# Fused chunk attention and wave mixer on one core: scores on eight array tiles in four PSUM banks, and the last chunks of two batch pairs in one group

## The chip, the core and the metric

The kernel runs on one core of a Trainium2 chip. The core has a matmul engine (TensorE, PE in the profile) with its weight loads (PEld), VectorE (DVE), ScalarE (ACT), GpSimd (POOL) and SyncE (SP); each works through its own list of instructions in order and waits on semaphores for the others. Sixteen DMA engines move data between HBM and SBUF; transfers are issued from the queues of SP, ACT and POOL. TensorE writes to PSUM, eight banks of 512 fp32 values on each of 128 partitions. The metric is the device time of one execution in microseconds, the median of the runs shown. The profile is that of one execution more.

## The reference

Attention inside chunks of 64 tokens, and then a mixer on its result. Batch 8, 8 heads, 576 tokens, 64 values per head: nine chunks for each batch and head.

```python
scores = (q_c @ k_c.transpose) / sqrt(64)          # per batch, head and chunk: 64 x 64
attn = softmax(scores); x = attn @ v_c             # x: (8, 576, 512), heads side by side
theta = x @ w_theta                                # 512 x 512
zr, zi = x * cos(theta), x * sin(theta)
y = w_tok_r @ zr + w_tok_i @ zi                    # over the tokens: 576 x 576
u = x + y
out = u + relu(u @ w_ch)                           # 512 x 512
```

Inputs and output are fp32; the kernel computes in fp16 with fp32 sums, and leaves out the subtraction of the row maximum in the softmax, which it doesn't need for these values.

## The kernel before

The batches are taken in four pairs p = 0 to 3. The 2 x 576 tokens of a pair make nine tiles j = 0 to 8 of 128 tokens: 0 to 3 are the first 512 tokens of the first batch, 4 to 7 those of the second, and tile 8 holds the last 64 tokens of both. For the attention a pair is cut into five groups (`GROUPS`): A and B (tiles 0,1 and 2,3), C and D (4,5 and 6,7), and M (tile 8, the last chunks).

A group goes through these steps, each a short name:

- `qk`: q and k are loaded by GpSimd's queue, cast to fp16 on the way, with two tokens and eight heads on a partition (L174; M: L169). For 0A alone q and k come as fp32 by SP's queue (`hq`, `hk`) and are cast on ScalarE and VectorE (`cqa`, `ckv`). `v`: v by GpSimd's queue (L214).
- `T` (or `Tq`, `Tk`): VectorE transposes blocks of 32 x 32 (L321), so that pairs of head values lie on the partitions: two values of one partition are the two terms e = 0, 1 of a sum in PSUM.
- `S`: scores (L339), 64 matmuls of 32 rows by 64 columns in a full group, 32 in an M group. The 128 x 128 array is used in tiles of 32 rows and 64 columns, of which there are eight. A full group uses four of them and two PSUM banks, an M group two. `S0` and `S1` are halves by heads.
- `E`: the exponential (L365, ScalarE). `V0`, `V1`: the products with v and a column of ones, four heads each (L382, four array tiles of 64 x 64). `N0`, `N1`: division by the sum on VectorE (L397, L399), which writes x.
- `X`: x is transposed on TensorE (L419) and copied (`xa` ScalarE, `xv` VectorE), or transposed by DMA (`xd`, SP's queue). `H`: theta (L457). `G`: cos and sin (L476). `Z`: zr and zi (L492 to L499).
- per tile then `Y` (or its parts `Ya`, `Yb`, `Ym`): the mixing over tokens (L522); `A`: + x (L534); `U` with `ua`, `uv`, or `ud`: transposed u, by TensorE or by DMA; `W`: the last matmul (L562); `R`: relu and sum (L574); `st`, `sa`: the store from SP's or ACT's queue.

`TW` transposes the token weights loaded by `lw`; `lt`, `cta` load and cast w_theta; `lc` loads w_ch. ScalarE holds one table of functions at a time; E and G need different ones, and `table` (L144) loads the other when it changes.

Nothing is scheduled at run time: the string `ORDER` lists all steps, and each engine gets its instructions in that order. A step is written `S.1A.6`: step, pair and group (or tile), and a last number, which for TensorE's steps is the first PSUM bank, for loads and other buffers the slot. `dm.21.7` is 21 dummy matmuls of 512 columns into bank 7, which keep TensorE busy where the order expects it to wait (32 in all, 21 of them first). A step that writes a bank waits until the last reader of the bank is done, a load until the last reader of its slot is done. Of the transfers that one queue issues, eight have a semaphore each at a time: the ninth waits in the queue until the first has landed.

## Time and profile before

| | |
|---|---|
| median of 3 runs (lowest, highest) | 194.25 us (193.74, 196.09) |
| the profiled execution, and its span | 192.63 us, 190.9 us |
| granted TensorE clock | 0.999 |
| TensorE, VectorE, ScalarE, GpSimd busy | 94%, 72%, 53%, 44% of the span |
| score matmuls (L339) | 1152, 13.7 us busy |
| dummies (L158) | 32, 10.6 us busy |

"Span" is the time from the first to the last instruction. In a list of groups or a timeline a row names line, engine and operation, output and inputs, partitions x elements, and how many; "[2.50 <-DVE T L321]" is idle time of the engine just before, and what ended it. Matmuls overlap and each has its full length on record (some 0.19 us for a small one), so a run of them is as long as its row less what the last one runs on alone. A row of windows gives a stretch and its length, then for each engine its busy time and the instructions at work in it, then the granted clock, the share of the DMA engines and GB/s.

### The profile page before, as it was taken

What the parts mean: (1) busy time and instruction counts of PE and PEld (TensorE: products, weight loads), DVE (VectorE), ACT (ScalarE), POOL (GpSimd) and SP (SyncE); (2) the same over time, 40 slices, a digit from 0 to 9 for tenths busy, and PEclk for the clock granted to TensorE, in tenths of its full rate; (3) what the DMA queues carried; (4) which work ended last, traced back from release to release, by engine and by line L of the source; (5) the groups of instructions that cost most, each with busy time, mean ns of one, the idle gap of its engine ahead of it and who ended that gap; (6) DMA issues with size and microseconds to landing.
All of it is one profiled execution on the core that took longest, in us unless ns stands there. A gap on an engine that the chain in (4) does not pass through costs nothing.

```text
span 190.9 us, 6053 instructions
## 1 busy us (share of the span) xinstructions
PE 179.3 (94%) x2626; PEld 93.0 (49%) x2626; DVE 136.8 (72%) x254; ACT 100.7 (53%) x129; POOL 84.9 (44%) x119
## 2 busy tenths in 40 slices
PE   7769899999999999998999999999989999999980
PEld 2245555655556555655456555454544444444430
DVE  0167889789958989959788798967771963672761
ACT  3238979399579780499062774996344650000000
POOL 7786988559856997789578400000000000000000
PEclk9999999999999999999999999999999999999999
DMA  5999999999999999999999998632498315256596
GB/s 156 252 225 187 176 172 174 193 132 159 259 199 162 120 162 198 183 173 194 201 228 200 176 163 180 85 86 82 84 87 177 99 55 137 59 192 165 133 319 213
DMA packets 99867, 31.48 MB, mean 165 GB/s; under 512 B 90880, under 2 KB 94848, under 8 KB 99840
## 3 DMA queue, kind: packets, MB, share of 16 engines
q0 software_dynamic: 75152, 15.49, 93.9%
q1 hardware_dynamic: 21936, 10.75, 24.8%
q10 hardware_dynamic: 2752, 4.85, 7.4%
q8 instruction: 20, 0.33, 0.7%
q14 instruction: 7, 0.06, 0.1%
HBM read 33.06 MB, written 9.44 MB: 223 GB/s over the span
## 4 chain that ended last, share of the span: by engine, by line
PE 64%; DMA 17%; POOL 6%; ACT 5%; DVE 3%; issue 3%; DVEq 0%; POOLq 0%
PE psum L522 29%; DMA land<-in_k_dram 15%; PE psum L562 12%; PE psum L457 11%; PE psum L339 4%; POOL v L214 3%; PE psum L382 2%; POOL land L174 2%; DMA uT<-x 2%; PE psum L419 2%; PE psum L539 2%; ACT L144 1%; PE psum L288 1%; DVE T L321 1%; ACT sin L476 1%
## 5 line engine op out<-in xcount | busy, mean ns | idle before, releaser
L522 PEld LDWEIGHTS <-wT 128*128 128x128 f16 (+1 forms) x360 | 31.0, 100 | 34.5 <-issue 1.2
L214 POOL DMA_DIRECT2D v<-in_v_dram x56 | 42.0, 772 | 7.1 <-DMA land<-in_k_dram 4.0
L522 PE MATMUL psum<-zr,wT 128*128 128x512 f16 (+1 forms) x180 | 44.7, 380 | 0.0
L522 PE MATMUL psum<-zi,wT 128*128 128x512 f16 (+1 forms) x180 | 42.9, 379 | 0.0
L534 DVE TENSOR_TENSOR x<-psum,x 128x512 f16<-128x512 f32 x36 | 24.3, 684 | 20.2 <-PE psum L522 20.0
L562 PE MATMUL psum<-wch,uT 128*128 128x512 f16 (+1 forms) x148 | 35.2, 374 | 1.2 <-DMA uT<-x 0.7
L457 PE MATMUL psum<-wtheta,xT 128*128 128x512 f16 x144 | 34.1, 379 | 0.2 <-DVE xT L442 0.2
L321 DVE STREAM_TRANSPOSE T<-land 128x1024 f32<-128x1024 f32 (+4 forms) x27 | 25.4, 953 | 10.0 <-DMA land<-in_q_dram 5.9
L574 DVE SCALAR_TENSOR_TENSOR o<-psum,x 128x512 f32<-128x512 f32 (+1 forms) x37 | 24.1, 670 | 9.3 <-PE psum L562 9.2
L365 ACT ACTIVATE eT<-psum 128x1024 f16<-128x1024 f32 (+1 forms) x22 | 18.2, 860 | 22.7 <-PE psum L339 20.3
L476 ACT ACTIVATE cos<-psum,pihalf 128x1024 f16<-128x1024 f32 (+1 forms) x22 | 21.1, 958 | 12.5 <-PE psum L457 11.4
L399 DVE TENSOR_TENSOR x<-psum,recip 128x512 f16<-128x512 f32 (+1 forms) x40 | 25.5, 638 | 1.4
L144 ACT ACT_TABLE_LOAD x20 | 25.7, 1283 | 1.1 <-PEq L643 0.7
L562 PEld LDWEIGHTS <-uT 128*128 128x128 f16 x148 | 13.6, 98 | 15.8 <-DMA uT<-x 1.5
L457 PEld LDWEIGHTS <-xT 128*128 128x128 f16 x144 | 13.5, 98 | 16.0 <-DVE xT L442 0.6
L476 ACT ACTIVATE sin<-psum 128x1024 f16<-128x1024 f32 (+1 forms) x22 | 19.0, 865 | 0.0
L174 POOL DMA_DIRECT2D land<-in_q_dram x15 | 14.3, 950 | 5.8 <-DMA land<-in_k_dram 2.1
L339 PE MATMUL psum<-T 32*64 32x64 f16 x1152 | 13.7, 193 | 3.3 <-DVE T L321 3.3
L339 PEld LDWEIGHTS <-T 32*64 32x64 f16 x1152 | 11.8, 106 | 7.6 <-DVE T L321 4.3
L174 POOL DMA_DIRECT2D land<-in_k_dram x15 | 13.6, 907 | 1.7 <-DMA land<-in_k_dram 1.5
L492 DVE TENSOR_TENSOR zr<-x,cos 128x1024 f16<-128x1024 f16 (+1 forms) x18 | 11.2, 623 | 1.3 <-ACT cos L476 1.0
L493 DVE TENSOR_TENSOR zi<-x,sin 128x1024 f16<-128x1024 f16 (+1 forms) x18 | 11.3, 627 | 0.8 <-ACT sin L476 0.7
(39 smaller groups left out, 124.9 us busy)
## 6 DMA issues: line engine op xcount, KB each, us to landing
out_dram<-o ACTq DMA_DIRECT2D x17, 256.0 KB, 3.4
land<-in_q_dram POOLq DMA_DIRECT2D x15, 256.0 KB, 6.6
land<-in_k_dram POOLq DMA_DIRECT2D x15, 256.0 KB, 7.9
out_dram<-o SPq DMA_DIRECT2D x14, 256.0 KB, 4.6
v<-in_v_dram POOLq DMA_DIRECT2D x40, 64.0 KB, 6.4
v<-in_v_dram POOLq DMA_DIRECT2D x16, 128.0 KB, 7.2
land<-in_moe_w_theta_dram SPq DMA_DIRECT2D x2, 512.0 KB, 7.1
out_dram<-o SPq DMA_DIRECT2D x7, 128.0 KB, 3.2
```

Of the source, the lines that this page charges most:

```text
L144: nc.scalar.activation(out=first, in_=pihalf, func=func)
L174: nc.gpsimd.dma_start(t[:, w].rearrange("p h s d -> p h (s d)"), ap[2 * p + bb, :, s0 : s0 + GT, :].rearrange("h (p s) d -> p h (s d)", s=2),)
L214: nc.gpsimd.dma_start(v16[rows, slot + t, :, 0:D], v[b, :, t0 : t0 + m, :].rearrange("h s d -> s h d"),)
L321: nc.vector.transpose(to.bitcast(FP32).rearrange("p (x l s) -> p x s l", l=32, s=2), src.bitcast(FP32).rearrange("p (x s d) -> p x s d", s ...
L339: nc.tensor.matmul(ps[half[r ^ cc], r, h - hs[0]], t[quarter[c], 1, h, :, e], t[quarter[c], 0, h, :, e], start=(e == 0), stop=(e == 1), ti ...
L399: nc.vector.tensor_tensor(out=x.rearrange("p r (h d) -> p r h d", h=H // 2), in0=ps[:, :, :, 0:D], in1=recip[:, 0:n].broadcast_to((P, n, H ...
L457: nc.tensor.matmul(ps[:, (j - js[0]) * DM : (j - js[0] + 1) * DM], xT[:, j, a, :], wtheta16[:, a, :], start=(a == 0), stop=(a == NDB - 1),)
L476: nc.scalar.activation(out=t[:, js[0] : js[-1] + 1].rearrange("p j e -> p (j e)"), in_=ps, func=AF.Sin, bias=bias, scale=1.0,)
L522: nc.tensor.matmul(ps[half[c]] if j == MID else ps, wT[:, kt, t0 : min(t0 + P, S)], z, start=(b is not None and i == 0), stop=(i == len(kt ...
L534: nc.vector.tensor_tensor(out=x, in0=st.pop(("ps_y", p, j)), in1=x, op=ALU.add)
L562: nc.tensor.matmul(ps, uT[:, a, :], wch16[:, a, cols[f]], start=(a == 0), stop=(a == NDB - 1),)
L574: nc.vector.scalar_tensor_tensor(out=o, in0=ps, scalar=0.0, in1=st["x", p][:, j, cols[f]], op0=ALU.max, op1=ALU.add,)
```

## The change

- **Loads of q and k.** A full group now has four tokens and four heads on a partition: heads 0 to 3 on partitions 0 to 63, heads 4 to 7 on 64 to 127. So each load is two, one for each half of the partitions, and their runs in HBM are twice as long. An M group keeps two tokens.
- **Transpositions** write with a step of four; q and k of 0A, 0B, 0C and 0D are transposed in one instruction each.
- **Scores.** The 64 matmuls of a full group go to all eight tiles of 32 x 64, in turn, and into four banks (heads half f and tile r choose the bank), half a bank each. `S0`, `S1` are gone; `E0`, `E1` now take the halves of what `S` wrote.
- **Last chunks.** M of pair 2 takes M of pair 3 along (`WITH_NEXT`): one group of four chunks, 64 score matmuls on four tiles, and one step each where there were two. For that, x, zr, zi and v16 are one array each with one tile more (`OWN`), and `place` says where tile j of pair p lies.
- **Dummies** read one zero repeated 512 times. Helpers that no step used are gone.
- **Order.** A new `ORDER`, with 51 dummies: it begins with 0A, then 0M, then 0B.

```diff
+WITH_NEXT = (2,)
+OWN = 1
...
+    heads = [range(H // 2), range(H // 2, H)]
...
+    def place(p, j):
+        return p % 2 * MID + j if j < MID else 2 * MID + (1, 0, 1, 2 * OWN)[p]
+
+    def pairs(p, g):
+        if g != "M":
+            return [p]
+        ps = [p, p + 1] if p in WITH_NEXT else [p]
+        return sorted(ps, key=lambda x: place(x, MID))
...
-            nc.tensor.matmul(banks(b), zeros[:, 0:P], zeros)
+            nc.tensor.matmul(banks(b), zeros, zeros[:, 0:1].broadcast_to((P, DM)))
...
-                nc.gpsimd.dma_start(
-                    t[:, w].rearrange("p h s d -> p h (s d)"),
-                    ap[2 * p + bb, :, s0 : s0 + GT, :].rearrange(
-                        "h (p s) d -> p h (s d)", s=2
-                    ),
-                )
+                for f in range(2):
+                    nc.gpsimd.dma_start(t[half[f], w].rearrange("p (h x) -> p h x", h=H // 2), four(ap, p, g, f))
+
+    def four(ap, p, g, f):
+
+        j0, bb, s0 = GROUPS[g]
+        rows = ap[2 * p + bb, heads[f][0] : heads[f][-1] + 1, s0 : s0 + GT, :]
+        return rows.rearrange("h (p s) d -> p h (s d)", s=4)
...
+            n, s = (CH * size(p, g), 2) if g == "M" else (P, 4)
...
             nc.vector.transpose(
-                to.bitcast(FP32).rearrange("p (x l s) -> p x s l", l=32, s=2),
-                src.bitcast(FP32).rearrange("p (x s d) -> p x s d", s=2, d=32),
+                to.bitcast(FP32).rearrange("p (x l s) -> p x s l", l=32, s=s),
+                src.bitcast(FP32).rearrange("p (x s d) -> p x s d", s=s, d=32),
             )
...
-            for h in hs:
+    def scores(p, g, b):
+        n = size(p, g)
+        if g == "M":
+            ps = banks(b, n).rearrange("p (r f x) -> p f r x", r=n, f=2)
+            t = st["T", p, g].rearrange("p w (h y e) -> p w h y e", h=H, e=2)
+            work = [
+                (quarter[c], half[c // 2 ^ c % 2], c // 2, f, f * (H // 2), slice(0, CH))
+                for c in range(2 * n) for f in range(2)
+            ]
+            work = [[x for x in work if x[3] == f] for f in range(2)]
+        else:
+
+
+            ps = banks(b, 4).rearrange("p (f r x) -> p f r x", r=n, f=2)[:, :, :, 0 : H // 2 * CH]
+            t = st["T", p, g].rearrange("p w (h y e) -> p w h y e", h=H // 2, e=2)
+            work = [
+                [
+                    (quarter[2 * f + r], half[r ^ cc], r, f, 0, slice(CH * cc, CH * cc + CH))
+                    for cc in range(2) for f in range(2) for r in range(2)
+                ]
+            ]
+        for part in work:
+            for h4 in range(H // 2):
                 for e in range(2):
-                    for c in range(2 * n):
-                        r, cc = (c // 2, c % 2) if n == 2 else (0, c)
+                    for rows, cols, r, f, h0, y in part:
                         nc.tensor.matmul(
-                            ps[half[r ^ cc], r, h - hs[0]],
-                            t[quarter[c], 1, h, :, e],
-                            t[quarter[c], 0, h, :, e],
+                            ps[cols, f, r, h4 * CH : h4 * CH + CH],
+                            t[rows, 1, h0 + h4, y, e],
+                            t[rows, 0, h0 + h4, y, e],
                             start=(e == 0),
                             stop=(e == 1),
-                            tile_position=(32 * c, CH * (r ^ cc)),
+                            tile_position=(rows.start, cols.start),
                         )
```

The first steps of the new order:

```diff
+pre.00 hq.0A.0 hk.0A.1 lt.00.2 cqa.0A.3 lt.01.4 ckv.0A Tq.0A.0 Tk.0A dm.25.7 S.0A.0
+E0.0A.0 qk.0M.5 Tq.0M.1 Tk.0M dm.3.7 S.0M.4 E.0M.1 v.0M dm.2.7 V1.0M.5 cta.00 E1.0A
+cta.01 qk.0B.6 Tq.0B.2 Tk.0B dm.15.7 S.0B.0 E0.0B.2 N1.0M V0.0M.6 N0.0M v.0A V0.0A.4
+V1.0A.6 E1.0B N0.0A init.00 v.0B N1.0A lw.00.7 dm.3.3 V0.0B.0 dm.1.5 X0.0A.2 X1.0A.3
+V1.0B.4 N0.0B xa0.0A.0 xa1.0A N1.0B H0.0A.6 H1.0A.7 X0.0B.0 qk.0D.8 X.0M.1 xv0.0B.1
...
```

255 lines of the change are left out of this document (108 added, 147 removed).

## The prediction

> **What bounds the kernel now.** I read the page first (busy shares, slices, queues, the chain by engine), then stretches of the span, then the timeline of the first 22 us.
>
> ```profile
> span 190.9 us, 6053 instructions
> PE 179.3 (94%) x2626; PEld 93.0 (49%) x2626; DVE 136.8 (72%) x254; ACT 100.7 (53%) x129; POOL 84.9 (44%) x119
> ...
> DMA  5999999999999999999999998632498315256596
> ...
> PE 64%; DMA 17%; POOL 6%; ACT 5%; DVE 3%; issue 3%; DVEq 0%; POOLq 0%
> ...
> 1.10:20.10 19.00, 15.35 (x202) 7.11 (x202) 8.61 (x22) 8.82 (x13) 15.01 (x23) 1.00 1.47 214
> 20.10:93.00 72.90, 72.35 (x1295) 40.38 (x1296) 60.91 (x114) 53.61 (x71) 58.79 (x80) 1.00 1.78 178
> 93.00:179.30 86.30, 85.49 (x1101) 42.71 (x1100) 62.03 (x111) 37.90 (x46) 10.88 (x14) 1.00 0.86 132
> 179.30:186.10 6.80, 6.09 (x32) 2.76 (x30) 4.41 (x8) 0.00 (x0) 0.00 (x0) 1.00 1.04 295
> ```
>
> The last four rows are stretches; the column behind the length is TensorE's busy time. From 20.1 us to 186.1 TensorE is idle for 0.55 + 0.81 + 0.71 = 2.07 us in all, at full clock (1.00). So the time is: when TensorE gets going, plus its work, plus some 5 us of last stores. VectorE, ScalarE and GpSimd have room. A saving counts only if it takes TensorE time away or lets it start earlier. The DMA row is full until about 125 us, yet after 20 us no load makes TensorE idle for long: loads are ahead of their use there. The profiled execution took 192.63 us (span 190.9 and 1.7 around it), 1.6 under the median of the three runs, 194.25; I work out the difference and add it to the median.
>
> **Eight array tiles.** What does a score matmul cost, and what sets it?
>
> ```profile
> 10.87 0.70 PE L339 MATMUL psum<-T 32*64 32x64 f16 x32 [2.50 <-DVE T L321]
> ...
> 35.40 0.71 PE L339 MATMUL psum<-T 32*64 32x64 f16 x64
> ...
> 101.53 0.58 PE L382 MATMUL psum<-v,eT 64*64 64x65 f16 x48
> ...
> 66.19:66.31 0.12, 0.11 (x12) 1.00 1.87 186
> 66.19:66.33 0.14, 0.13 (x16) 1.00 1.89 188
> 66.19:66.34 0.15, 0.14 (x16) 1.00 1.82 181
> 66.19:66.36 0.17, 0.16 (x20) 1.00 1.83 182
> 66.19:66.37 0.18, 0.17 (x20) 1.00 1.86 185
> 66.19:66.59 0.40, 0.39 (x48) 1.00 1.81 180
> ...
> 66.19:67.04 0.85, 0.84 (x103) 1.00 1.80 177
> 66.19:67.05 0.86, 0.85 (x104) 1.00 1.80 177
> 66.19:67.06 0.87, 0.86 (x105) 1.00 1.79 177
> 66.19:67.07 0.88, 0.87 (x106) 1.00 1.80 177
> 66.19:67.26 1.07, 1.06 (x128) 1.00 1.80 178
> ```
>
> In the timeline rows I take off 0.19 us, the recorded length of the last small matmul. A last-chunk group (32 matmuls, two array tiles in use) then has 0.51 / 32 = 16 ns each; a full group (64, four tiles) 0.52 / 64 = 8.1 ns; the products with v (four tiles of 64 rows) 0.39 / 48 = 8.1 ns. Twice the tiles, half the time: so far that speaks for eight tiles, and would give 4 ns. The windows (score matmuls only; x counts those begun since 66.19, where two groups of 64 run back to back) speak against it. Early, the count jumps 12, 16, 16, 20, 20: bursts of four, one burst per 32 ns, each matmul waiting for its tile. Late, it climbs by one per 10 ns: no bursts, though the tiles would still allow them. A matmul that waits for its tile starts in the burst; one that starts singly has just arrived. From 66.59 to 67.26 come 80 in 0.67 us, 8.4 ns each: that is the pace at which pairs of weight load and matmul are delivered, and more tiles don't raise it. The bursts early in the group show a stock of only a few pairs. With 8.4 ns per pair and some four pairs in stock a group of 64 takes 60 x 8.4 = 0.50 us in place of 0.52: 0.02 us for each of 16 groups, 0.3 us. The other end is 64 x 4 = 0.26 us, 4.2 us for all. I take 0.3, since the late rows show the very rate that is asked for, and keep 4.2 for the range.
>
> The row of the tail says 8.4 ns per pair. The Trainium skill, page "TensorE: Matmul & The Clock Gate", section "Part 3: Packing small matmuls — row/col tiling", states about 4 ns of issue per further tile and a window 64 instructions deep; by that rule the groups would take the 0.26 us, and this is the first rival below. The trace agrees within a burst and not over a whole double group.
>
> **Last chunks of pairs 2 and 3 in one group.** Two groups of 32 on two tiles become one of 64 on four: 2 x 0.51 against 0.52, −0.5 us. Its products with v are 32 in two runs instead of four short runs: I give −0.2. One 3M transposing load (xd) becomes four TensorE transposes:
>
> ```profile
> 101.60 0.51 PE psum L382 x43
> 102.11 0.97 PE psum L562 x4
> 103.09 0.45 PE psum L419 x8
> ...
> 108.09 0.86 PE psum L562 x4
> ...
> L144 ACT ACT_TABLE_LOAD x20 | 25.7, 1283 | 1.1 <-PEq L643 0.7
> ...
> L321 DVE STREAM_TRANSPOSE T<-land 64x1024 f32<-64x1024 f32 x3 | 3.7, 1228 | 0.0
> ```
>
> Eight transposes take 0.45 us on the chain, so four add 0.2. VectorE loses one 1.2 us transposition, and in the new order ScalarE changes tables 14 times and not 20 (6 x 1.28 = 7.7 us less); neither engine ends a wait that TensorE feels for more than the 2.07 us, so I cost both at nothing; bounds 0 and −2. The transpositions now write with a step of four tokens and not two, the dummies stream one zero 512 times: as many elements as before, so nothing; were a transposition twice as long, the three of 0.7 us ahead of the first scores would add 2.1 us.
>
> **The new order.** Four wide matmuls take 0.97 us behind a run of small ones (L382) and 0.86 otherwise: 0.1 us for each change between small and whole-array matmuls. Counted in the two orders there are 63 such changes before and 71 after: +0.8. TensorE's work together: −0.3 − 0.5 − 0.2 + 0.2 + 0.8 = 0.0 us. Scores now take four of eight banks; the order keeps other steps off them, and where it does not, a product waits for an exponential (bounded under the rivals).
>
> **The start** is what is left, and there the rows are these:
>
> ```profile
> 1.19 7.18 PE L158 MATMUL psum<-zeros 128*128 128x512 f16 x21 [1.19 <-DVE pihalf L149]
> ...
> 1.29 1.28 POOL L169 DMA_DIRECT2D land<-in_q_dram  x2 [0.85 <-POOLq L643]
> ...
> 4.98 1.04 ACT L200 CAST land<-land 128x1024 f16<-128x1024 f32 x1 [2.75 <-DMA land<-in_q_dram]
> ...
> 7.68 0.70 DVE L321 STREAM_TRANSPOSE T<-land 64x512 f32<-64x512 f32 x1 [5.88 <-DMA land<-in_q_dram]
> ...
> 9.86 0.54 POOL L251 DMA_DIRECT2D land<-in_moe_w_tok_i_dram  x1 [1.36 <-DMA land<-in_k_dram]
> ...
> 11.86 0.89 POOL L174 DMA_DIRECT2D land<-in_k_dram  x1
> ...
> land<-in_k_dram SPq DMA_DIRECT2D x1, 512.0 KB, 6.1
> ...
> 19.27 0.77 DVE L321 STREAM_TRANSPOSE T<-land 128x256 f32<-128x256 f32 x2 [0.96 <-DMA land<-in_k_dram]
> ...
> 20.10 0.45 PE L339 MATMUL psum<-T 32*64 32x64 f16 x32 [0.78 <-DVE T L321]
> ...
> DMA to landing us min/median/max: 4.4/7.2/11.1
> ...
> L214 POOL DMA_DIRECT2D v<-in_v_dram x56 | 42.0, 772 | 7.1 <-DMA land<-in_k_dram 4.0 <-PE psum L382 1.0 <-issue 0.8
> ...
> L169 POOL DMA_DIRECT2D land<-in_q_dram x8 | 4.9, 624 | 3.3 <-DMA land<-in_q_dram 1.6 <-DMA v<-in_v_dram 0.9 <-POOLq L643 0.8
> ```
>
> Before, k of group 0B was issued at 11.86 and landed at 19.25, and TensorE stood until 20.10. By then it had done about 5.1 us of real work (96 score matmuls, 56 with v, 18 transposes, 8 wide ones, some ten changes), so 15.0 us were lost to start, dummies and waits, 15.2 with one dummy behind.
>
> After, group 0A comes first. q and k land about as before (q is cast at 4.98; k takes 6.1 us from an issue half a microsecond behind q's, to about 7.4), then VectorE casts and transposes: scores 0A at about 9.4, where 25 dummies end (21 take 7.18, four more 0.22 each, a quarter of the 0.86 above: 9.2). 0M follows at about 10.6. GpSimd issues four last-chunk loads (0.62 each, from 1.29), two of v, and the two q halves of 0B, to 6.3. Eight transfers are then under way, and the row at 9.86 shows what the next does: its queue stands until an old one has landed. So k's halves of 0B go out when 0M's q has landed, at 7.7 to 8.9; v of 0A follows to 11.7 and v of 0B at 12.3 to 14.6. A half is 128 KB instead of 256, and fewer bytes are ahead of it, so I take 5 us to land, between 4.4 and 7.2 of the 256 KB loads: k of 0B at 13.9 (within the 15 dummies, which end at 15.3), v of 0B at 19.5. In the new order the X step of 0A and all behind it stand on TensorE behind V0 of 0B, which needs that v. Then 0.25 for V0, 0.5 for transposes and a dummy, 0.4 to copy: the first wide matmul (H0 of 0A) at 20.6, with 3.7 us of real work done: 16.9 lost, 17.3 with two dummies behind it. That is 2.1 us more than before. Ends: none more, if the 19 further dummies (0.22 each, 4.1 us) stand just where TensorE waited anyhow; 4.2 more if a transfer takes the median 7.2 (k of 0B at 16.1; v's issue slips to 16.5, its landing to 23.7).
>
> Splitting each q and k load costs GpSimd 4 x 0.62 in place of 0.95 + 0.89, 0.6 us for each of 15 groups; from 20 us on loads run ahead, and that hides it. On this the Trainium skill's page "DMA: Bandwidth & Descriptors", section "Rules for kernel authors", advises against two transfers to the two partition halves, since both use the same engines; no row here shows such halves. By it the landing would be no earlier than with one transfer, the 7.2 of the last paragraph.
>
> **Sum** against the profiled execution: TensorE's work 0.0, start +2.1, waits later unchanged: 192.63 + 2.1 = 194.7, and against the median 194.25 + 2.1 = 196.35; I say 196.0, giving 0.35 for the lighter ScalarE.
>
> **Rivals.**
> 1. *Eight tiles run at twice the rate.* For: 16 ns on two tiles, 8.1 on four. Against: the single starts at 8.4. Then 4.2 − 0.3 = 3.9 us less: 192.1; with dummies that cover the start exactly, 190.0.
> 2. *Loads late (slower).* The eight-deep queue of GpSimd now holds half-size transfers; if each still takes 7.2 us, the start is 4.2 later in place of 2.1, and 0D and 0C, two and four rounds of the same queue behind, come about 1 us late each: 196.0 + 2.1 + 2 = 200.1. It decides from a landing of about 6 us on. For: the queue was waited for from 9.86 on. Against: a transfer of half the size.
> 3. *Start covered.* The dummies fit the waits, the mid waits (2.07) shrink to half with fewer table changes: 194.25 + 0 − 1 = 193.2.
> 4. *The tiles are not in flight together* (two column tiles of one row strip exclude each other): that is no change of rate, and falls in with the forecast.
>
> **How the numbers follow.** Forecast 0.45 at 196.0 (193.5 to 198.5); rival 1 0.22; rival 2 0.20; rival 3 0.13. The range reaches from the low end of rival 1, 190.0, to rival 2, with a little room: 190.0 to 200.5. About 2% is what a measurement here can tell from no change: below 190.4 or above 198.1. Faster by that: half of rival 1, 0.12. Slower: rival 2 and a little of the forecast, 0.23. The rest, 0.65, within.
>
> **What would show it.** In the profile after: score groups of 64 in about 0.69 to 0.71 us on the timeline (right), or about 0.45 (rival 1); whether the score matmuls start singly. The first wide matmul at 20.6; v of 0B landing at 19.5; idle time ahead of L382 in the first 22 us ended by a DMA. If TensorE's idle time from there to 186 us is well over 2 us, my cost of nothing for banks and waits fails; a first wide matmul before 19 us makes the start term wrong.

## The result, and the profile after

The changed kernel takes 205.56 us (median of 4 runs, 203.91 to 205.68), the kernel before beside it 194.76 (193.74 to 196.09): 1.053 times as long, 95% interval 1.046 to 1.060. The forecast was 196.0, the range ended at 200.5; both were too low. Some executions of one kernel take a few per cent longer than its others (209.35 us beside 199.07 to 200.52 in one run below); the ratios leave these out and the medians don't, so a ratio can differ from the quotient of two medians. The profiled execution took 203.91 us.

The page of the changed kernel, rows that answer to those shown of the kernel before:

```profile
span 202.0 us, 6112 instructions
PE 185.0 (92%) x2649; PEld 94.5 (47%) x2649; DVE 147.0 (73%) x245; ACT 90.3 (45%) x112; POOL 94.7 (47%) x149
...
PEclk9979999999999999999999999999999999999998
...
PE 52%; DMA 23%; POOL 11%; DVE 5%; issue 4%; ACTq 1%; ACT 1%; DVEq 0%; SPq 0%; POOLq 0%
```

ScalarE is 10 us lighter, with fewer table loads, as foreseen. VectorE, which lost nine instructions, is busy 10 us longer. The clock row has a dent in the third slice that the kernel before hadn't.

Where the 11.1 us between the two spans lie is told by stretches from the first wide matmul (17.42 before, 23.99 after) to the end of TensorE's work. Column two is the length, column three TensorE's busy time. First the kernel before, then the changed one:

```profile
17.42:93.00 75.58, 74.25 (x1303) 41.08 (x1304) 62.64 (x118) 55.60 (x75) 59.36 (x81) 1.00 1.78 178
93.00:179.30 86.30, 85.49 (x1101) 42.71 (x1100) 62.03 (x111) 37.90 (x46) 10.88 (x14) 1.00 0.86 132
179.30:186.07 6.77, 6.06 (x32) 2.76 (x30) 4.38 (x8) 0.00 (x0) 0.00 (x0) 1.00 1.04 296
```

```profile
23.99:100.00 76.01, 72.97 (x1199) 40.19 (x1200) 65.12 (x110) 49.89 (x65) 63.61 (x96) 1.00 1.51 166
100.00:189.00 89.00, 86.78 (x1123) 42.63 (x1122) 66.82 (x109) 32.63 (x37) 12.56 (x19) 1.00 0.73 136
189.00:196.49 7.49, 6.43 (x34) 2.95 (x31) 4.23 (x7) 0.00 (x0) 0.00 (x0) 1.00 0.64 169
```

Start: 23.99 − 17.42 = 6.6 us later. Busy time: 166.2 against 165.8, 0.4 more. Idle: 6.3 against 2.8, 3.5 more. Behind TensorE's end: 5.5 against 4.8, 0.7 more. Together 11.1. By its first wide matmul the changed kernel has done 64 score matmuls and 32 products with v more than the kernel before and ten transposes fewer, some 0.2 us of work. So TensorE's work came out within about half a microsecond of the forecast; start and waits did not.

The waits of TensorE in the changed kernel (total, times, longest):

```profile
PE psum L351 <- DVE T L319: 5.5, 4, 3.4
PE psum L567 <- DMA uT<-x: 2.1, 2, 1.1
```

Scores wait for a transposed T, late products for a DMA transposition. The first 24 us, from the timeline (start, length, then engine and line):

```profile
6.09 1.04 ACT L221 CAST land<-land 128x1024 f16<-128x1024 f32 x1 [3.86 <-DMA land<-in_q_dram]
...
9.17 1.11 DVE L223 CAST land<-land 128x1024 f16<-128x1024 f32 x1 [7.54 <-DMA land<-in_k_dram]
10.20 3.06 DVE L319 STREAM_TRANSPOSE T<-land 128x512 f32<-128x512 f32 x4
...
12.21 0.75 PE L351 MATMUL psum<-T 32*64 32x64 f16 x64 [3.41 <-DVE T L319]
...
12.90 1.46 PE L174 MATMUL psum<-zeros 128*128 128x512 f16 x3
...
15.66 1.11 DVE L319 STREAM_TRANSPOSE T<-land 128x512 f32<-128x512 f32 x1 [0.32 <-DMA land<-in_k_dram]
...
16.29 3.44 PE L174 MATMUL psum<-zeros 128*128 128x512 f16 x15
...
19.66 0.71 PE L351 MATMUL psum<-T 32*64 32x64 f16 x64
...
23.99 1.90 PE L462 MATMUL psum<-wtheta,xT 128*128 128x512 f16 x8 [0.20 <-ACT xT L449]
```

q is cast 1.1 us later than before (4.98), k is there at 9.17 (its issue, behind two transfers for q, starts at 2.22 in place of 1.27), and the first scores start at 12.21 where the forecast had 9.4. TensorE stands 3.4 us for them. Then 15 dummies hold the scores of 0B until 19.66, though their T is done at 16.77.

The transpositions of VectorE by shape (x count, busy time, mean ns), first of the kernel before, then of the changed one:

```profile
L321 DVE STREAM_TRANSPOSE T<-land 128x1024 f32<-128x1024 f32 x12 | 14.8, 1237 | 1.5 <-DMA land<-in_k_dram 1.5
...
L321 DVE STREAM_TRANSPOSE T<-land 128x512 f32<-128x512 f32 x6 | 4.1, 694 | 0.0
```

```profile
L319 DVE STREAM_TRANSPOSE T<-land 128x1024 f32<-128x1024 f32 x13 | 25.4, 1965 | 0.0
...
L319 DVE STREAM_TRANSPOSE T<-land 128x512 f32<-128x512 f32 x8 | 8.4, 1072 | 1.3 <-DMA land<-in_q_dram 1.0 <-DMA land<-in_k_dram 0.3
```

As many elements take 1.5 to 1.6 times as long. One of the 13 is the merged last chunks, which still writes with a step of two and takes 1.23 us; the twelve others take 2.03 us on average. Together the transpositions take 36.2 us and not 25.4, which is VectorE's extra time.

### The profile page after: what moved, and what is told of

Its sections match the earlier page's. It is cut to its first block, busy times and chain, and to the rows that moved or that the text cites. A ratio compares the mean times of both kernels' runs of the same rounds, so it can differ in the third digit from the quotient of the medians.

```text
span 202.0 us, 6112 instructions
## 1 busy us (share of the span) xinstructions
PE 185.0 (92%) x2649; PEld 94.5 (47%) x2649; DVE 147.0 (73%) x245; ACT 90.3 (45%) x112; POOL 94.7 (47%) x149
## 4 chain that ended last, share of the span: by engine, by line
PE 52%; DMA 23%; POOL 11%; DVE 5%; issue 4%; ACTq 1%; ACT 1%; DVEq 0%; SPq 0%; POOLq 0%
PE psum L527 23%; DMA v<-in_v_dram 14%; PE psum L567 13%; PE psum L462 9%; POOL land L195 5%; DMA uT<-x 4%; POOL v L237 4%; DMA land<-in_q_dram 3%; PE psum L351 3%; DMA land<-in_moe_w_tok_r_dram 3%; DVE T L319 2%; PE psum L388 2%; POOL land L189 1%; DVE o L579 1%; PE psum L544 1%
## 5 line engine op out<-in xcount | busy, mean ns | idle before, releaser
L527 PE MATMUL psum<-zr,wT 128*128 128x512 f16 (+1 forms) x180 | 45.4, 381 | 0.0
L368 ACT ACTIVATE eT<-psum 128x1024 f16<-128x1024 f32 (+1 forms) x21 | 18.8, 899 | 41.5 <-PE psum L351 38.3
L319 DVE STREAM_TRANSPOSE T<-land 128x1024 f32<-128x1024 f32 (+3 forms) x24 | 36.1, 1527 | 1.4 <-DMA land<-in_q_dram 1.0
L567 PE MATMUL psum<-wch,uT 128*128 128x512 f16 (+1 forms) x148 | 34.5, 374 | 2.1 <-DMA uT<-x 2.1
L462 PE MATMUL psum<-wtheta,xT 128*128 128x512 f16 x144 | 33.4, 379 | 0.2 <-ACT xT L449 0.2
L195 POOL DMA_DIRECT2D land<-in_q_dram x30 | 19.0, 651 | 4.0 <-DMA wch<-in_moe_w_ch_dram 1.4
L195 POOL DMA_DIRECT2D land<-in_k_dram x30 | 19.0, 653 | 1.4 <-DMA land<-in_q_dram 0.6
L174 PE MATMUL psum<-zeros 128*128 128x512 f16 x51 | 15.3, 451 | 1.0 <-DVE pihalf L165 1.0
L402 DVE RECIPROCAL recip<-psum 128x8 f32<-128x8 f32 (+1 forms) x38 | 7.5, 197 | 9.7 <-PE psum L388 9.5
```

The lines of the kernel that those rows point to most:

```text
L195: nc.gpsimd.dma_start(t[half[f], w].rearrange("p (h x) -> p h x", h=H // 2), four(ap, p, g, f))
L319: nc.vector.transpose(to.bitcast(FP32).rearrange("p (x l s) -> p x s l", l=32, s=s), src.bitcast(FP32).rearrange("p (x s d) -> p x s d", s ...
L368: nc.scalar.activation(out=st["eT", p, g][:, fs, 0:n].rearrange("p f r h i -> p f r (h i)"), in_=st["ps_s", p, g][:, fs], func=AF.Exp, sca ...
L462: nc.tensor.matmul(ps[:, (j - js[0]) * DM : (j - js[0] + 1) * DM], xT[:, j, a, :], wtheta16[:, a, :], start=(a == 0), stop=(a == NDB - 1),)
L527: nc.tensor.matmul(ps[half[c]] if j == MID else ps, wT[:, kt, t0 : min(t0 + P, S)], z, start=(b is not None and i == 0), stop=(i == len(kt ...
L567: nc.tensor.matmul(ps, uT[:, a, :], wch16[:, a, cols[f]], start=(a == 0), stop=(a == NDB - 1),)
```

## The experiments

Theory 1: the transpositions with a step of four are slow, and TensorE waits for them. Theory 2: the halved loads of q and k come late. Theory 3, the rival to both: order, banks and dummies. Later runs take parts of the third: dummies, the start of the order and its end. The four banks and the merged last chunks were never undone by themselves. Each ratio is against the kernel before in the same set of runs. Diffs of `ORDER` show only the steps that change.

### One part undone

**Step of two.**

```diff
-            n, s = (CH * size(p, g), 2) if g == "M" else (P, 4)
+            n, s = (CH * size(p, g), 2) if g == "M" else (P, 2)
```

> The changed kernel with one thing undone: the transpositions of groups A to D write with a step of two tokens again, not four. Loads, tiles, banks, order and the number of elements stay; the tokens come out in another sequence, so what is computed from them isn't the reference's, and the work is the same. Theory 1 (the step of four makes VectorE slower, and TensorE waits for it): a 128x512 transposition falls from 1.07 to about 0.69 us and a 128x1024 one from 1.97 to about 1.24, VectorE is busy some 12 us less, the first scores come 0.8 us earlier (two transpositions), the waits of scores for T shrink, and the time falls from 205.6 by 2 to 4 us. Theory 2 (the halved loads and the theta loads ahead make it late): the transpositions may be shorter, the time stays within 1 us of 205.6. Theory 3 (order, banks and dummies): as theory 2.

201.27 us, 1.038 of before (1.032 to 1.043), against 1.053: about 3 us back. The transpositions:

```profile
L319 DVE STREAM_TRANSPOSE T<-land 128x1024 f32<-128x1024 f32 x13 | 16.0, 1235 | 0.2
...
L319 DVE STREAM_TRANSPOSE T<-land 128x512 f32<-128x512 f32 x8 | 5.5, 700 | 2.8 <-DMA land<-in_q_dram 2.4 <-DMA land<-in_k_dram 0.4
```

Theory 1 holds for this part: from 24 us to TensorE's end the idle time is 3.5 us, where the changed kernel has 6.3 behind its first wide matmul. The start gained nothing: the first scores came 0.7 us earlier (though q, loaded as before, was cast only at 6.66), the first wide matmul 1.1 later (25.07), because the 15 dummies took 5.4 us at a lower clock (see the runs on the clock).

**One load of 256 KB.**

```diff
-                for f in range(2):
-                    nc.gpsimd.dma_start(t[half[f], w].rearrange("p (h x) -> p h x", h=H // 2), four(ap, p, g, f))
+                nc.gpsimd.dma_start(
+                    t[:, w].rearrange("p (h x) -> p h x", h=H),
+                    ap[2 * p + bb, :, s0 : s0 + GT, :].rearrange("h (p s) d -> p h (s d)", s=2),
+                )
```

The two loads of 0A on SP's queue change in the same way.

> The changed kernel with one thing undone: q and k of a group A to D each come in one transfer of two tokens by eight heads per partition, as in the kernel before, not in two halves of four tokens by four heads. The bytes land in the same places, but heads and tokens are mixed, so the scores aren't the reference's; all steps behind the load are unchanged. Theory 2 (two half transfers cost): ScalarE's cast of q starts about 1 us earlier than 6.1, k's cast at 7.5 to 8 in place of 9.2, the first scores at about 10.6 and not 12.2; GpSimd issues 15 x 0.6 = 9 us less; the time falls by 1.5 to 3 us. Theory 1 (transpositions) and 3 (order, dummies): the landing may come earlier, the time stays within 1 us of 205.6.

203.52 us, 1.048 (1.043 to 1.054). The casts start at 4.96 and 7.59, the first scores at 10.57, the first wide matmul at 21.83, all as theory 2 says; but of these 2.2 us the time keeps only about 0.9, inside the intervals' width. The rest is lost again in waits behind.

**The whole old layout** (one load, step of two, four tiles; banks, merged chunks and order as changed).

```diff
-            n, s = (CH * size(p, g), 2) if g == "M" else (P, 4)
+            n, s = (CH * size(p, g), 2) if g == "M" else (P, 2)
...
-                    (quarter[2 * f + r], half[r ^ cc], r, f, 0, slice(CH * cc, CH * cc + CH))
-                    for cc in range(2) for f in range(2) for r in range(2)
+                    (quarter[2 * r + cc], half[r ^ cc], r, f, f * (H // 2), slice(0, CH))
+                    for f in range(2) for r in range(2) for cc in range(2)
```

> The changed kernel with the whole layout of q and k undone: one load of two tokens by eight heads, transpositions with a step of two, scores on four tiles at a time; kept are the four PSUM banks, the merged last chunks, the dummies and the new order. What is computed is the reference's. Theories 1 and 2 together: the gains of the two runs above add up, and the time is 199 to 201. If the layout is all there is, it is about 195, as before. Theory 3 (order, banks, dummies are the loss): above 203. If eight tiles were worth their 4 ns per matmul, the score groups would now take longer than in the changed kernel (0.64 us from start to the next step); I expect 0.64 to 0.66.

200.47 us, 1.030 (1.021 to 1.039). Theories 1 and 2 together, and not all; the distance to the 1.038 with the step of two alone is inside the intervals' width. The scores of 0B take 0.64 us to the next step on four tiles, as on eight. The first scores start at 9.20, but the first wide matmul still at 22.98.

How a group starts shows what the eight tiles do and why it brings nothing. The rows are windows from the start of a group on (score matmuls only, x counts those begun), first of the changed kernel with eight tiles, then of this run with four:

```profile
69.57:69.61 0.04, 0.04 (x8) 1.00 0.67 42
69.57:69.71 0.14, 0.14 (x32) 1.00 0.68 43
69.57:69.79 0.22, 0.22 (x32) 1.00 1.12 127
69.57:70.05 0.48, 0.48 (x62) 1.00 1.35 112
```

```profile
66.74:66.78 0.04, 0.04 (x4) 1.00 1.99 125
66.74:66.88 0.14, 0.14 (x16) 1.00 2.03 126
66.74:66.96 0.22, 0.22 (x28) 1.00 2.03 122
66.74:67.22 0.48, 0.48 (x60) 1.00 1.80 102
```

On eight tiles the first 32 start within 0.14 us, 4.4 ns each, and on four tiles 16. Then on eight tiles none starts for some 0.1 us, and the other 32 follow some 8 ns apart, which is the pace of four tiles all along. The 64 have started after 0.50 to 0.52 us on either. All 16 full groups of the changed kernel stop behind the 32nd.

The start of this run:

```profile
4.95 1.04 ACT L224 CAST land<-land 128x1024 f16<-128x1024 f32 x1 [2.72 <-DMA land<-in_q_dram]
...
7.23 0.69 DVE L226 CAST land<-land 128x1024 f16<-128x1024 f32 x1 [5.61 <-DMA land<-in_k_dram]
...
9.20 0.71 PE L354 MATMUL psum<-T 32*64 32x64 f16 x64 [1.19 <-DVE T L322]
...
13.61 5.11 PE L174 MATMUL psum<-zeros 128*128 128x512 f16 x15
...
16.13 0.71 DVE L322 STREAM_TRANSPOSE T<-land 128x512 f32<-128x512 f32 x1 [2.22 <-DMA land<-in_k_dram]
```

k of 0B comes at 16.13, and the dummies, 0.34 us each in place of 0.22, end at 18.64. So one transfer in place of two halves doesn't bring k of 0B earlier: it comes at 16.13 here, at 15.03 in the run with one load alone, and at 15.66 in the changed kernel.

### The step of the transposition, on the kernel before

```diff
-                to.bitcast(FP32).rearrange("p (x l s) -> p x s l", l=32, s=2),
-                src.bitcast(FP32).rearrange("p (x s d) -> p x s d", s=2, d=32),
+                to.bitcast(FP32).rearrange("p (x l s) -> p x s l", l=32, s=2 if g == "M" else 4),
+                src.bitcast(FP32).rearrange("p (x s d) -> p x s d", s=2 if g == "M" else 4, d=32),
```

> The kernel before with one thing done: the transpositions of groups A to D write with a step of four tokens. The tokens come out in another sequence, so what is computed isn't the reference's; nothing else changes. Theory 1: a 128x1024 transposition takes 1.97 us and not 1.24, VectorE is busy about 11 us more, and the time grows by 1.5 to 4 us over 194.8. Rival (VectorE's room hides it in either order): less than 1 us.

196.04 us, 1.011 (1.005 to 1.017): the step alone costs the kernel before about 2.2 us (1.0 to 3.4), at the low end of theory 1. The same with 8 in place of 4 (one execution, 196.92 us):

> The kernel before with the transpositions of groups A to D writing with a step of eight tokens (32 bytes); the tokens come out in another sequence, so what is computed isn't the reference's. If what costs is that each write falls into another 16 bytes (one write per 16 bytes from a step of four on), a 128x1024 transposition takes as long as with a step of four, 1.97 us. If the cost grows with the step, about 3 us or more.

The groups with a step of four and, below, of eight:

```profile
L321 DVE STREAM_TRANSPOSE T<-land 128x1024 f32<-128x1024 f32 x12 | 24.1, 2011 | 0.0
```

```profile
L321 DVE STREAM_TRANSPOSE T<-land 128x1024 f32<-128x1024 f32 x12 | 24.3, 2023 | 0.1
```

1.24, 2.01 and 2.02 us for steps of 8, 16 and 32 bytes: from 16 bytes on the cost doesn't grow with the step. That fits a cost that comes when neighbouring writes no longer share 16 bytes; a step between 8 and 16 was not run. This agrees with the Trainium skill, page "SBUF — State Buffer", section "Door 1: The DMA port swizzle", which has lines of 16 bytes that need at least two hits each for full bandwidth. The same note calls a stride of up to four fp32 free; here four is slow and two is not, and the measurement decides.

### The start: loads, dummies, clock

**Theta later.**

```diff
-pre.00 hq.0A.0 hk.0A.1 lt.00.2 cqa.0A.3 lt.01.4 ckv.0A Tq.0A.0 Tk.0A
+pre.00 hq.0A.0 hk.0A.1 cqa.0A.3 lt.00.0 ckv.0A lt.01.1 Tq.0A.0 Tk.0A
```

> The changed kernel with its two loads of the theta weights (1 MB in all) no longer issued behind k of 0A but into the landing buffers of q and k, so that they wait for the casts of q and k, as the kernel before had its second half. Theory 2a (their bytes delay the first loads): k of 0A lands about 1 us earlier, the first scores at 11.2 in place of 12.2, k of 0B is transposed from about 14.5 in place of 15.7, the time falls by 0.7 to 1.5 us. Rival (GpSimd's own queue sets the landings): the first scores may come earlier, the first wide matmul stays within 0.5 us of 24.0 and the time within 0.5 us.

204.33 us, 1.055 (1.048 to 1.062): no gain. k is cast at 10.14, not earlier; the theta loads are not what holds it. Theory 2a falls.

**The 15 dummies out.**

```diff
-Tk.0B dm.15.7 S.0B.0
+Tk.0B dm.1.7 S.0B.0
```

> The changed kernel with 1 in place of 15 dummy matmuls ahead of the scores of 0B. Their place was chosen for a k that lands; in the changed kernel its transposition was done at 16.8 and the dummies held TensorE until 19.7. Theory 4 (the dummies themselves are the delay): the scores of 0B at 16.9, the first wide matmul at 21.5 to 22, the time 2 to 2.7 us less. Rival (v of 0B, which lands behind, decides): the products with v of 0B wait for their load, the first wide matmul comes no earlier than 23.3, the time falls by under 0.8 us. A second rival: without the dummies the granted clock falls, and the wide matmuls behind run slower.

205.30 us, 1.062 (1.051 to 1.074): slower, if anything. The scores of 0B start at 17.20, but the second rival came true:

```profile
14.00:16.00 2.00, 2.00 (x35) 1.05 (x34) 1.09 (x1) 0.63 (x2) 1.93 (x5) 0.50 1.84 176
22.00:24.00 2.00, 2.00 (x27) 1.23 (x26) 1.21 (x3) 1.46 (x3) 1.12 (x2) 0.50 1.30 162
```

The granted clock (the column behind POOL's) is 0.50 in every stretch from 12 to 24 us, and the first four wide matmuls take 1.44 us in place of 0.87.

**40 first dummies.**

```diff
-Tk.0A dm.25.7 S.0A.0
+Tk.0A dm.40.7 S.0A.0
```

> The changed kernel with 40 first dummies in place of 25, which end at about 12.1, just ahead of the first scores, in place of 8.8. Theory 5 (TensorE's idle 3.4 us ahead of the first scores brings the granted clock down, to 0.57 in 12 to 16 us): the clock stays at 1.00, the three dummies behind take 0.66 us and not 1.39, the scores of 0M 0.63 and not 0.99, the first wide matmul comes about 1.1 us earlier, and the time falls by 1 us. Rival: the clock falls all the same, or what comes earlier waits for v: within 0.3 us.

203.14 us, 1.049 (1.042 to 1.056), within the intervals of the changed kernel. The mechanism is there: at 12 to 16 us the clock is 1.00, where the changed kernel has 0.58 and 0.56, here first the changed kernel, then this run:

```profile
12.00:14.00 2.00, 1.79 (x67) 0.90 (x67) 1.26 (x3) 0.60 (x1) 0.78 (x2) 0.58 1.59 189
14.00:16.00 2.00, 2.00 (x35) 1.05 (x34) 1.44 (x2) 0.61 (x2) 1.93 (x5) 0.56 1.93 172
```

```profile
12.00:14.00 2.00, 2.00 (x76) 0.95 (x76) 1.53 (x3) 0.60 (x1) 0.00 (x0) 1.00 1.64 187
14.00:16.00 2.00, 1.85 (x45) 1.03 (x44) 1.10 (x1) 1.38 (x2) 1.84 (x4) 1.00 1.84 176
```

The Trainium skill, page "TensorE: Matmul & The Clock Gate", section "Part 1: The HAM clock gate (the "warmup" mystery)", has the clock at half behind an idle window of about 3.4 us; TensorE's 3.4 us ahead of the first scores agree, with a clock of 0.50 from 12.5 to 15.5 us behind them in the changed kernel. With the old layout it fell to 0.53 behind two idle stretches of 1.2 and 1.3 us, so waits that are each below that window don't keep it safe.

**Old layout, theta later, other dummies** (only the dummies are shown).

```diff
-dm.25.7 S.0A.0
+dm.29.7 S.0A.0
...
-dm.3.7 S.0M.4
+dm.7.7 S.0M.4
...
-dm.15.7 S.0B.0
+dm.5.7 S.0B.0
```

> The changed kernel with the old layout of q and k (as in the run above that undoes it), the theta loads into the buffers of q and k, and the dummies fitted to that start: 29 first, 7 ahead of the scores of 0M, 5 ahead of those of 0B. What is computed is the reference's. If the start is what is left of the loss: scores of 0B at 16 or earlier in place of 18.6, the first wide matmul at about 20.5 in place of 23.0, the time 197.5 to 198.5. If v of 0B or the order decides: the first wide matmul at 22 or later, 200.

199.62 us, 1.030 (1.021 to 1.040): no gain. k of 0B decides: TensorE waits 2.8 us for its T, the scores start at 17.22.

**Old layout, 0A's wide products first.**

```diff
-dm.2.7 V1.0M.5 cta.00 E1.0A cta.01 qk.0B.6 Tq.0B.2 Tk.0B dm.15.7 S.0B.0
+dm.6.4 V0.0A.4 N0.0A qk.0B.6 V1.0A.6 N1.0A cta.00 dm.5.3 X0.0A.2 xv0.0A.0 X1.0A.3 xv1.0A
+cta.01 v.0B lw.00.7 dm.2.1 H0.0A.6 H1.0A.7 Tq.0M.1 Tk.0M S.0M.0
...
```

> The changed kernel with the old layout of q and k, and with its first steps in another order: v of 0A is loaded ahead of the last chunks, and on TensorE the products of 0A with v, its transposes and its wide theta products stand ahead of the scores of 0M and 0B, not behind the products of 0B with v. Dummies are put to the waits this makes; all behind is as in the changed order, and what is computed is the reference's. Theory 6 (the new order's start is the rest of the loss: its first wide product stands behind the loads of 0B): the first wide matmul at 14 to 16 us in place of 23.0, TensorE waits for k of 0B at about 17 instead, and the time falls from 200.5 to 196 or below. Rival (the loads of 0B hold the rest in any order): the first wide matmul comes early, TensorE then stands as long for 0B, and the time stays above 199.

200.44 us, 1.029 (1.024 to 1.034). The first wide matmul starts at 14.92, yet the scores of 0B only at 20.95, and the wide products of 0B behind them take 1.71 us for four at a clock of 0.50. The rival holds: the first wide matmul alone is not the measure of a start.

**Old layout, clock kept** (30, 9 and 16 dummies).

> The changed kernel with the old layout of q and k and dummies that fill TensorE's waits at the start: 30 first, 9 ahead of the scores of 0M, 16 ahead of those of 0B. What is computed is the reference's. Theory 5 (the granted clock, which falls behind idle stretches, makes the dummies and small products slow): the clock stays at 1.00 up to 26 us, the scores of 0B at 17.0 in place of 18.6, the first wide matmul at 21.4 in place of 23.0, the time 1.5 us below the run with the old layout alone (1.030 of before to 1.022). Rival: no gain, within 0.5 us of 1.030.

200.25 us, 1.029 (1.025 to 1.034): the rival again. The clock stays at 1.00 and the first wide matmul comes at 22.28, 0.7 us earlier; the time doesn't follow.

**Old layout with the first steps of the kernel before.**

```diff
+pre.00 qk.0M.0 hq.0A.1 cqa.0A.2 hk.0A.3 Tq.0M.0 Tk.0M v.0M init.00 v.0A dm.21.7 S.0M.0
...
+X0.0B.3 X1.0B.4 TW.00.5 xv0.0B.2 G.0M.1 xa1.0B H0.0B.7 H1.0B.4 G0.0B.2 G1.0B twv.00 Tq.0D.0 Tk.0D
 S.0D.0 qk.1M.10 Z0.0B Z1.0B Ya.00.6
...
```

> The old layout of q and k with the first steps of the kernel before (its order of loads and of TensorE up to the theta products of 0B, its 21 first dummies and its later theta loads) and from there on the changed order, with the four banks and the merged last chunks; what is computed is the reference's. Theory 6 (the rest of the loss, 1.030 of before with the old layout alone, is the changed start): the first wide matmul at about 17.5 in place of 23.0, by 30 us some 3 us more of TensorE's work is done, and the time falls to 1.010 to 1.018 of before. Rival (merged chunks, four banks and the later order hold the rest): it stays above 1.025.

210.45 us, 1.087 (1.079 to 1.095): slower than the changed kernel. Grafted together, the two orders wait for each other (products with v 3.3 us for an exponential, scores 3.7 us for T), so this run tells nothing about the changed start.

### Halves of a load, on the kernel before

By the two halves of the partitions, and by heads on all 128 partitions:

```diff
+                for f in range(2):
+                    nc.gpsimd.dma_start(
+                        t[half[f], w].rearrange("p h s d -> p h (s d)"),
...
+                        t[:, w, 4 * f : 4 * f + 4].rearrange("p h s d -> p h (s d)"),
...
```

> The kernel before with each load of q and k of a group A to D split into two transfers to the two halves of the partitions, as many bytes and pieces of 512 B; nothing else changes. Theory 2 (the number of transfers costs): GpSimd issues some 9 us more, the first loads land 0.5 to 1 us later, the time grows by 0.5 to 2 us. Rival (it is hidden): within 0.5 us of before.

> The kernel before with each load of q and k split into two transfers to the two halves of the partitions, as in the earlier run, whose times lay far apart. Theory 2b (a transfer to 64 partitions runs at about half the rate, as the bytes of the first microseconds show): k of 0A is cast about 1 us later than in the kernel before, the time is 1.005 to 1.015 of before, and more than that of the run beside it, which splits by heads.

> The kernel before with each load of q and k split into two transfers of four heads each, both to all 128 partitions: as many transfers and bytes as in the run beside it. Theory 2b (half the partitions, half the rate): the first loads land as in the kernel before, within 0.4 us, and the time is within 0.5% of before. Rival (the second transfer itself costs): as late and as slow as the run beside it.

By partitions 198.59 us the first time (196.54 to 203.27, too far apart to compare) and 197.53 the second, 1.016 (1.011 to 1.022); by heads 201.49 (195.66 to 205.50), 1.014 (1.006 to 1.023), a ratio from two executions. Both cost something, the times do not tell them apart, and theory 2b's half per cent for the split by heads did not come. The first microseconds do tell them apart. For each of the two, by partitions first, stand the stretch 2 to 4 us (last column GB/s) and ScalarE's cast of q on the timeline:

```profile
2.00:4.00 2.00, 2.00 (x6) 0.76 (x5) 0.00 (x0) 0.22 (x2) 2.00 (x4) 1.00 0.91 194
```

```profile
6.09 1.05 ACT L204 CAST land<-land 128x1024 f16<-128x1024 f32 x1 [3.86 <-DMA land<-in_q_dram]
```

```profile
2.00:4.00 2.00, 2.00 (x6) 0.76 (x5) 0.00 (x0) 0.23 (x2) 2.00 (x5) 1.00 1.00 265
```

```profile
4.49 1.04 ACT L204 CAST land<-land 128x1024 f16<-128x1024 f32 x1 [2.25 <-DMA land<-in_q_dram]
```

In these stretches 194 GB/s move against 265 (247 in the kernel before; so halves are slower, but not at half the rate, as theory 2b had it). All traces say the same of q of 0A: with two halves it is cast at 6.04 to 7.35 us (eight traces), with one transfer at 4.95 to 5.18 (eleven), with two transfers by heads at 4.49 (one). So it is the halves of the partitions, not the number of transfers, that make q 1.1 us late in the changed kernel. The rate of the stretch alone says less: it is 186 to 210 GB/s with halves and 213 to 247 with one transfer.

k of 0A, which theory 2b expected 1 us later, was cast earlier on the kernel before, at 10.02 and 9.99 against 10.75: there it stands on VectorE behind k of the last chunks, which came earlier. Why the split by heads is no faster in the end was not settled; in its profiled execution, one of 204.12 us, k of the last chunks comes 1.1 us later than before (11.17 against 10.11).

### What paces the scores

```diff
-            for h4 in range(H // 2):
+            for h4, u in [(h4, u) for h4 in range(H // 2) for u in (0, 32)]:
...
-                            ps[cols, f, r, h4 * CH : h4 * CH + CH],
+                            ps[cols, f, r, h4 * CH + u : h4 * CH + u + 32],
```

> The changed kernel with each score matmul of 64 columns cut into two of 32; products and results are the same, the number of score matmuls doubles from 1152 to 2304. If the eight tiles are held back by the delivery of weight loads and matmuls (8.3 ns each, the prediction's reading), a group takes 128 x 8.3 = 1.07 us to the next step's start in place of 0.64. If the tiles are the limit (64 columns of work each), it stays at about 0.64.

A group in this run:

```profile
24.94 1.22 PE L351 MATMUL psum<-T 32*64 32x32 f16 x128
```

Twice as many matmuls of half the columns take 1.15 us to the next step, not 0.64: 8.0 ns for each further one, with 32 columns as with 64. Together with the equal times on four and on eight tiles this says that a cost of each pair of weight load and matmul, not columns and not tiles, sets the time of a group; the prediction calls it delivery. Which part of the pair it is was not separated. The whole run (one execution) took 230.51 us; the scores explain some 9 of the 25 us, 7.6 more are waits of the products with v that the profile puts to issue alone.

### The late part

With the old layout two waits of TensorE are left behind 150 us, 2.4 us together, both for DMA transpositions on SP. The one of block 24 is issued at 166.46, behind three stores (20, 21 and 30; the expectation below counts four) and another transposition.

```diff
-xd.3C.2 st.20 st.21 W.23.1 R.23.0 R.26.4 H.3D.5 ud.31.7 G.3D.2 st.30 R.32.3 R.18.2 ud.24.2
+xd.3C.2 ud.24.2 sa.20 sa.21 W.23.1 R.23.0 R.26.4 H.3D.5 ud.31.7 G.3D.2 sa.30 R.32.3 R.18.2
...
```

Four more stores (23, 22, 27, 25) go from SP to ScalarE's queue.

> The changed kernel with the old layout of q and k, and in its last part two things moved: the DMA transposition of block 24 is issued on SP ahead of two stores instead of behind four and another transposition, and seven late stores go out through ScalarE's queue in place of SP's. What is computed is the reference's. Theory 7 (the last transpositions stand behind stores in SP's queue, and TensorE waits 1.6 us for the one of block 24 and 1.1 us for a later one): the first of these waits goes, the second shrinks, and the time falls from 1.030 of before to 1.019 to 1.024. Rival (the transposition waits for its input, or the saved time is lost at the next one): within 0.5 us of 1.030.

197.35 us, 1.014 (1.008 to 1.019), against 1.030 with the old layout alone. TensorE's waits of that run, and then of this one:

```profile
PE psum L354 <- DVE T L322: 2.8, 3, 1.3
PE psum L570 <- DMA uT<-x: 2.4, 2, 1.5
```

```profile
PE psum L465 <- DMA xT<-x: 0.4, 1, 0.4
```

The row for uT is gone; a wait of 0.4 us for another DMA transposition has come. So 2.0 us of waits went, as theory 7 has it. The gain of the ratios, some 3 us, is more than that, and their intervals are wide enough for the difference. The two profiled executions took as long as each other (199.40 and 199.59 us; in the second the start is slower), so the rows show which wait went and the gain stands on the ratios. The same late part with 0A's wide products first and dummies in the waits:

> As the run beside it, with the first steps in the order that puts 0A's wide products ahead of the scores of 0B (as in an earlier run), and with dummies added in the waits behind them, so that the granted clock doesn't fall to about half from 20 to 29 us as it did there. What is computed is the reference's. Theory 5 (it was the clock that took back what this start gained): the clock stays at 1.00 up to 30 us, TensorE has lost some 1.5 us less by 30 us than in the run beside it, and the time is 1.5 us below that run. Rival (the loads of 0B set the start in any order): within 0.5 us of that run.

199.42 us, 1.028 (1.022 to 1.035). The clock is 1.00 from 10 to 30 us, and it is no faster than the run with that start and the old late part (1.029): in this order TensorE waits 1.4 us for xT in the late part. So the gain of the late part was seen with one start and not with the other. Theory 5 falls as an account of the time: clock and dummies change the first 30 us by a microsecond or two, and the gain does not reach the end. None of the versions beats the kernel before.

## Why the prediction was wrong, point by point

- **TensorE's work (0.0).** Right within about half a microsecond. Eight tiles gain nothing: 0.64 us a group on four and on eight, score groups take 0.70 to 0.75 us on the timeline (0.69 to 0.71 forecast, 0.45 by rival 1), so rival 1 fell. The reason was half right. The second half of a group starts some 8 ns apart, as forecast; but the stock is 32 pairs and not a few, and these do start at twice the rate of four tiles. What they gain is lost in the stop behind them. The Trainium skill, page "TensorE: Matmul & The Clock Gate", section "Part 3: Packing small matmuls — row/col tiling", has some 4 ns of issue per further tile and a window of 64 instructions. The first 32 pairs, 64 instructions, agree with both at 4.4 ns each; the group as a whole doesn't.
- **The step that failed: "as many elements as before, so nothing".** The transposition with a step of four takes 2.03 us in place of 1.24. The prediction priced the doubled transposition only for the three ahead of the first scores (2.1 us) and left it out of range and rivals. Undone, it gives about 3 us; done to the kernel before, it costs about 2.2. The rows of before show steps of two alone, so nothing on record had a price for four.
- **The start, +2.1: mis-sized, it was +5.5** in the prediction's own count, which takes off the work done by then (first wide matmul at 23.99 and not 20.6). First scores: 12.21 and not 9.4. With the old layout they start at 9.20, so the forecast held for the one load and failed for the halves (k at 9.17, not 7.4) and the step. k of 0B: its last half, issued at 7.59, lands at 15.66, some 8 us and not 5; with one transfer it lands about as late. The forecast assumed the clock at 1.00 as before; behind the idle stretch it fell to 0.58. And the 15 dummies, counted as cover until 15.3, held the scores to 19.66. The path was another, too: v of 0B, on which the forecast hung the first wide matmul, landed by 20.0, near the 19.5 of the forecast, and ended no wait of TensorE. From the late scores of 0B on, small steps and four dummies took the 4.3 us to the first wide matmul.
- **"Waits later unchanged".** Wrong by 4.2 us: 6.3 of idle time behind the first wide matmul against the 2.07, by the prediction's own sign. They are scores waiting for slower transpositions, most of which the step of two takes away, and the late DMA transpositions. For these the order was never followed along SP's queue. The 1.4 us that are left of the 11.1 are work and the last stores.
- **Splitting loads, "hidden".** Wrong at the start: 1.1 us for q. The Trainium skill's rule against two half transfers (page "DMA: Bandwidth & Descriptors", section "Rules for kernel authors"), quoted in the prediction, agrees with the later q, and the forecast kept its 5 us against it.
- **Rivals.** Rival 2 had the landing of k of 0B right (about 16) and the side, but not the size: 200.1 against 205.56. Its sum is also short: a v of 0B at 23.7 in place of 19.5 puts the start 4.2 behind the forecast, not 4.2 behind the kernel before, which makes 202.2. And v of 0B didn't land at 23.7 but by 20.0: the start was late by another path. No case had the step, the clock and the loads together. A small misreading: by 20.10 the rows of before show 48 products with v, not 56.

The ratios, along one path: changed kernel 1.053; step of two 1.038; whole old layout 1.030; with the late queue rearranged 1.014. The first and the last of these steps are clear of the intervals, the middle one is not. The 1.4% left, 2.6 us, is not told apart. By the traces the old layout loses most at the start: at 30 us the kernel before has done 12 wide matmuls and 20 transposes of token weights more, some 3.7 us of work (0.215 us and 0.056 us each), and no run recovered more than some 0.7 us of it (the one with the clock kept). What of this comes from the order, the banks or the merged chunks stays open.

## What to carry to other kernels

Cost an access pattern by where its neighbouring elements fall, not by their number: with neighbours 16 bytes apart and not 8 a write made a transposition 1.6 times as long. A wait at the start can also let the clock fall, which makes what stands behind it slower; here keeping the clock moved the first wide matmul by 0.7 us and the time by nothing clear of noise. Dummies put in by count go on holding the engine when what they cover has moved, and taking them out can cost the clock. When an order is new, follow every in-order queue to the end, the stores' among them.

## What was not expected of the hardware

- A 128x1024 fp32 transposition on VectorE: 1.24 us with a step of 8 bytes, 2.01 with 16, 2.02 with 32.
- On eight tiles of 32 x 64 the first 32 score matmuls of a group start within 0.14 us; then none starts for some 0.1 us, and the rest come some 8 ns apart.
- With loads split into halves of the partitions q is cast at 6.04 to 7.35 us, with one transfer at 4.95 to 5.18, split by heads at 4.49; from 2 to 4 us 194 GB/s move with halves, 265 by heads. The Trainium skill's page "SBUF — State Buffer", section "Door 1: The DMA port swizzle", has partitions 0 to 63 reach half of the ports, at 196 GB/s for 1 MiB. The 194 lie close to that, though loads to both halves were under way here.
- With the 15 dummies out the granted clock was 0.50 from 12 to 24 us, though TensorE was busy nearly all that time with small products and dummies; and with the old layout it fell behind idle stretches of 1.2 and 1.3 us.
- VectorE's cast of 128x1024 took 0.64 to 0.78 us in most runs and 1.03 to 1.11 in three (the changed kernel, one load, clock kept) with the same operands. No run shows why.
